# Attention with a computed position bias and two MLPs: scores in four PSUM banks, bias rows in runs of 512 columns

## The chip, the core and the metric

The kernel runs on one core of a Trainium2 chip. The metric is the device time of one execution in microseconds (us), from the first to the last instruction with the launch around it, as the median of several runs. The profile is one more execution of the same program, taken by the hardware profiler; its span is the time from its first to its last instruction.

The engines are TensorE (PE; its weight loads are listed apart as PEld), VectorE (DVE), ScalarE (ACT), GpSimd (POOL) and SyncE (SP), which issues the DMAs. Each engine works through its own queue in order.

## The reference

Attention over 2 batches, 8 heads, 576 positions and a head size of 64, with a bias that a small network makes of the distance of two positions; then two MLPs of 512 to 2048 to 512 over the 1152 tokens.

```python
scores = scale * np.matmul(q, k.transpose(0, 1, 3, 2))
x = (log1p(abs(pos[:, None] - pos[None, :])) / log1p(max(pos[:, None], 1)))[..., None]
bias = np.maximum(x @ w1 + b1, 0.0) @ w2            # hidden 32, one row per head
scores = scores + bias.transpose(2, 0, 1)[None]
attn = softmax(scores)                              # over the keys
x = (attn @ v), heads side by side: 1152 x 512
h = x @ w_in;  g = where(h > 0, h, exp(min(h, 0)) - 1);  x = g @ w_out      # first MLP
h = x @ w_in;  g = max(h, 0) + log1p(exp(-abs(h)));      x = g @ w_out      # second MLP
```

The MLP weights come as float64 and are turned into pairs of float32 parts on the chip. A product in full precision is made of three matmuls of split operands (high by high, high by low, low by high).

## The kernel before

**Attention.** The 576 query positions are worked in five blocks: first the last 64 positions of both batches together (block 0), then four blocks of 128 (blocks 1 to 4). A unit is one block, one batch and one pair of heads: 36 units, of which 4 belong to block 0. For a unit `scores` (L634) writes two 128x576 score tiles, `soft` (L667) adds the bias on DVE while it takes the maximum, `expo` does the exponential on ACT, `turn` transposes on PE, `e_hi` and `e_lo` split the result into two float16 parts, `av` multiplies by v, and the `fin_` steps normalise and split.

**Scores.** 576 columns of float32 are more than one PSUM bank (512 columns) holds. The tile `ps3` has three banks. The two heads of a unit use the upper and the lower 64 rows of the PE array side by side: head 0 writes 512 columns to bank 0, head 1 writes 512 to bank 2, and the 64 columns that are left of each go to the two ends of the middle bank (L658) in one full-height matmul of 128 columns, for which a zero-padded copy `kz` of the key tails is loaded (`load_tail`) and split (`z_hi`, `z_lo`). So a unit of blocks 1 to 4 is six matmuls of 64 rows by 512 columns in three pairs (L656) and three of 128 columns (L658). Block 0 has twice as many.

**Bias.** For eight groups s of 16 query rows in a block, four tiles `y` (L510 on POOL, L512 on DVE) hold the hidden layer, 576 columns each. `bias_mm` (L518) multiplies them by w2 in four column strips of the array, in two halves of 288 columns, into `pb`, two PSUM banks; `bias_ev` (L535) evicts 576 columns in one ACT instruction (L539) into one of two `sg` buffers; `bias_out` (L541) sends it by one DMA (L546) to the bias tile, which `soft` reads. Eight groups by four blocks make 32 of these; block 0 has four groups with a plainer form of `y` and matmul (L504, L506, L521).

**Weights.** While attention runs, DVE, ACT and POOL turn the first MLP's weights from float64 into two parts (L241 to L274), 32 half-tiles of 512 columns, and the MLP's matmuls (L1264, L1308) begin as soon as their first weights and rows are there.

**Order.** Every step is a task with an engine, a cost and dependences. A list `RANK` gives each task's priority; a planner (`Order.forward`) plays the engines through and writes the tasks out in the order that results, so each engine's queue, SP's too, is fixed when the program is built. The table `ON` says which engine does a task that two could do: `YP` the 144 `y` tiles, `WP` the first step of a weight half, `KHP`, `KG`, `QHP`, `QP` the splitting of k and q. `rotates("pb", 1)`, `rotates("sg", 2)` and `rotates("ps", 1)` say how many buffers there are of `pb`, `sg` and the score tile: a new group or unit may be written when the last reader of the buffer is done, which for the score tile are both `soft` steps of the unit before.

Of the kernel before, what the change touches and what calls it, by code (L numbers as in the profile page):

```python
# [157 lines left out]
]  # L158

HOLD = dict(A=0.10, V=0.11, G=18.49, T=0.00, D=19.64)  # L160

ON = dict(
    KHP="AVAVVVVAAA",
    KG="VVVVVVVVVV",
    QHP="VAAAAVVAVVAAVVVAAAAA",
    QP="VGVVGVVVVGGGVGGGGVGG",
    WP="GVVGGVGVVVGGGVVVVVGVVVVVGGGVVGVVGGVGVGGVGGVGVVVGVGGVGGVGVVGVGVGG",
# [1233 lines left out]
```

## Time and profile before

| | us |
|---|---|
| median of 3 runs | 591.74 (591.17 to 592.08) |
| the profiled execution | 593.84 |
| its span | 592.1 |
| PE busy in the span | 572.1 (97%) |
| DVE busy | 436.6 (74%) |
| ACT busy | 408.0 (69%) |
| POOL busy | 117.7 (20%) |

The shares of the whole span are averages over stages that differ: attention with the bias and the weights fills about the first 190 us, and from about 190 us on the MLP matmuls run. A stretch has to be looked at by itself, engine by engine. A PE that is listed as busy is not thereby at its peak, since pipelined matmuls overlap: what a matmul costs is the distance from its start to the next one's start.

### The profile page before, as it was taken

Reading aid. Unit: us, or ns where it says so; the run is one execution under the profiler, and the core shown is the slowest. Engines: PE = TensorE matmul, PEld = TensorE weight load, DVE = VectorE, ACT = ScalarE, POOL = GpSimd, SP = SyncE. Lnnn points to the kernel's source line nnn. Section 1 sums busy time; section 2 is a strip of 40 time slices with the busy share of each in tenths; the row PEclk is TensorE's granted clock in tenths of the full one; section 3 lists DMA queues with packets and bytes.
Section 4 is the critical chain, followed back from the end, with each engine's and each line's share of the span. In section 5 each row is a group of like instructions: output and inputs, shape, how many; then the busy total and the mean of one; then the engine's idle time right before and its main releaser. Section 6 shows DMA issues by size and latency. Waiting matters only on the chain.

```text
span 592.1 us, 12610 instructions
## 1 busy us (share of the span) xinstructions
PE 572.1 (97%) x5002; PEld 491.4 (83%) x5002; DVE 436.6 (74%) x872; ACT 408.0 (69%) x798; POOL 117.7 (20%) x159
## 2 busy tenths in 40 slices
PE   8489999999999999999999999999999999999997
PEld 5256777777878888888889999998888888899996
DVE  7799999899999999999974699999972222332222
ACT  7678798888997766767745777687865444565453
POOL 3047767648300010010200020211110000000000
PEclk9989999999999999999999999999999999999999
DMA  8842843315201444444450045434500000020001
GB/s 303 260 115 77 217 116 104 82 42 168 63 2 41 139 130 156 143 151 142 148 164 1 2 148 169 144 110 145 161 15 1 0 1 1 0 108 1 0 2 53
DMA packets 19355, 56.63 MB, mean 96 GB/s; under 512 B 2144, under 2 KB 2528, under 8 KB 19040
## 3 DMA queue, kind: packets, MB, share of 16 engines
q1 hardware_dynamic: 19296, 55.82, 30.9%
q8 instruction: 39, 0.64, 0.4%
q14 instruction: 20, 0.16, 0.1%
HBM read 41.66 MB, written 2.36 MB: 74 GB/s over the span
## 4 chain that ended last, share of the span: by engine, by line
PE 85%; DMA 5%; ACT 4%; DVE 4%; issue 1%; POOL 0%; SPq 0%; DVEq 0%; ACTq 0%; POOLq 0%
PE ph L1264 33%; PE ps L1308 33%; PE tp L702 5%; PE ps L656 4%; PE pa L727 4%; PE pb L527 3%; DMA vr<-in_vt_dram 2%; PE ps L658 2%; DMA bias<-sg 1%; DVE y L512 1%; DVE et L711 1%; DVE e L672 1%; ACT e L689 1%; ACT sg L539 1%; ACT et L706 1%
## 5 line engine op out<-in xcount | busy, mean ns | idle before, releaser
L1264 PE MATMUL ph<-xh,wh 128*128 128x512 f32 (+2 forms) x384 | 127.6, 332 | 0.5 <-DVE t L1280 0.4
L1264 PE MATMUL ph<-xl,wh 128*128 128x512 f32 (+2 forms) x384 | 127.2, 331 | 0.0
L1264 PE MATMUL ph<-xh,wl 128*128 128x512 f32 (+2 forms) x384 | 127.1, 331 | 0.0
L1308 PE MATMUL ps<-g,wh 128*128 128x256 f32 (+2 forms) x384 | 94.3, 332 | 0.5 <-DVE xl L1316 0.5
L1308 PE MATMUL ps<-wh,g 128*128 128x512 f32 x288 | 91.9, 385 | 0.0
L1282 DVE SCALAR_TENSOR_TENSOR t<-ph,t 128x512 f32<-128x512 f32 (+2 forms) x48 | 26.7, 557 | 88.0 <-ACT t L1276 87.9
L510 POOL TENSOR_SCALAR y<-tpk,nbp 128x576 f32<-128x576 f32 x88 | 73.4, 849 | 34.8 <-PE pb L527 28.7
L1264 PEld LDWEIGHTS ph<-xh,wh 128*128 128x128 f32 x384 | 72.1, 188 | 5.9 <-DVE t L1280 0.5
L1264 PEld LDWEIGHTS ph<-xl,wh 128*128 128x128 f32 x384 | 72.1, 188 | 5.0
L1264 PEld LDWEIGHTS ph<-xh,wl 128*128 128x128 f32 x384 | 72.1, 188 | 4.8
L249 POOL TENSOR_SCALAR w<-w 128x512 f32<-128x512 f32 x30 | 28.4, 946 | 227.1 <-ACT w L241 164.7
L1308 PEld LDWEIGHTS ps<-g,wh 128*128 128x128 f32 x384 | 66.6, 188 | 5.6 <-DVE xl L1316 0.7
L1289 DVE TENSOR_TENSOR g<-t,g 128x512 fp32r<-128x512 f32 (+2 forms) x96 | 57.1, 596 | 18.6 <-ACT g L1286 17.7
L1286 ACT CAST g<-t 128x512 fp32r<-128x512 f32 (+2 forms) x96 | 48.9, 510 | 27.9 <-DVE t L1282 15.7
L1308 PE MATMUL ps<-g,wl 128*128 128x512 f32 (+2 forms) x192 | 63.5, 331 | 0.0
L1308 PEld LDWEIGHTS ps<-wh,g 128*128 128x128 f32 x288 | 54.0, 187 | 10.3
L1274 ACT ACTIVATE t<-ph 128x512 f32<-128x512 f32 (+2 forms) x48 | 23.6, 492 | 56.2 <-PE ph L1264 56.1
L711 DVE SCALAR_TENSOR_TENSOR et<-tp,et 128x512 f16<-128x512 f32 x81 | 54.0, 682 | 3.9 <-ACT et L706 3.6
L689 ACT ACTIVATE e<-e,mx 128x576 f32<-128x576 f32 x72 | 55.5, 775 | 1.3 <-DVE mx L672 1.2
L1308 PE MATMUL ps<-wl,g 128*128 128x512 f32 x144 | 55.5, 385 | 0.0
L706 ACT ACTIVATE et<-tp 128x512 f16<-128x512 f32 x81 | 46.2, 595 | 12.2 <-PE tp L702 11.6
L702 PE MATMUL tp<-ident,e 128*128 128x128 f32 x324 | 46.6, 278 | 3.3 <-DVE et L711 1.6
(137 smaller groups left out, 1050.2 us busy)
## 6 DMA issues: line engine op xcount, KB each, us to landing
r<-in_wa_dram SPq DMA_DIRECT2D x32, 512.0 KB, 3.7
r<-in_wb_dram SPq DMA_DIRECT2D x32, 512.0 KB, 3.6
bias<-sg SPq DMA_DIRECT2D x32, 288.0 KB, 3.4
vr<-in_vt_dram SPq DMA_DIRECT2D x2, 1152.0 KB, 11.5
sp<-sg SPq DMA_DIRECT2D x8, 288.0 KB, 3.3
out_dram<-o SPq DMA_DIRECT2D x9, 256.0 KB, 2.0
kr<-in_kt_dram SPq DMA_DIRECT2D x4, 512.0 KB, 8.7
qr<-in_qt_dram SPq DMA_DIRECT2D x8, 256.0 KB, 5.4
```

The costliest lines, as they stand in the source:

```text
L249: eng.tensor_scalar(wf, wf, F64_HUGE, F64_TINY, op0=ALU.min, op1=ALU.max)
L510: eng.tensor_scalar(y, tpk[:, b0 : b0 + S], BIG, nbp[:, qd : qd + 1], op0=ALU.min, op1=ALU.max)
L656: nc.tensor.matmul(sc[:, 1024 * x : 1024 * x + 512], q[r], kp[n][r, bb, hp], start=i == 0, stop=i == last)
L689: nc.scalar.activation(e, e, AF.Exp, bias=mxs[u][:, x : x + 1], scale=-1.0, accum_out=sums[u - hp][:, h : h + 1])
L702: nc.tensor.transpose(tp[:, r], e[:, t * P : (t + 1) * P], ident)
L706: nc.scalar.activation(et[:, 0], tps[g, k].rearrange("p t i -> p (t i)"), AF.Copy, scale=2.0**14)
L711: nc.vector.scalar_tensor_tensor(et[:, 1], tp, 2.0**14, et[:, 0], op0=ALU.mult, op1=ALU.subtract)
L1264: nc.tensor.matmul(in_fours(ps), a[:, kk], in_fours(x[:, kk]), start=n == 0, stop=n == 3 * KT - 1)
L1282: nc.vector.scalar_tensor_tensor(t[0], ps, 0.0, t[0], op0=ALU.max, op1=ALU.add)
L1286: nc.scalar.copy(g[0], t[0])
L1289: nc.vector.tensor_sub(g[1], t[0], g[0])
L1308: self.nc.tensor.matmul(in_fours(self.acc(m, c, j)), a, in_fours(x), start=f == 0 and n == 0 and not two, stop=f == FT - 1 and n == 2 and ...
```

## The change

1. The score tile becomes two tiles `ps4` of two banks each. Each head's 576 columns are two halves of 288, one per bank. `kz`, `load_tail`, `z_hi` and `z_lo` go; `kp` holds all 576 columns of the keys, and each key load is 1152 columns wide instead of 1024. A unit of blocks 1 to 4 is now twelve matmuls of 64 rows by 288 columns, in six pairs.
2. `pb` shrinks from two banks to one; scores and `pb` together hold five banks as before. In blocks 1 to 4 the rows of the eight groups, 8x576 columns, are laid end to end and cut into nine runs of 512 (`PIECES`): runs 0 and 8 are one piece each, runs 1 to 7 two pieces (64+448, 128+384, 192+320, 256+256 and back). `y`, the matmuls, the eviction and the DMA are issued once per piece. Block 0 keeps its four groups, in halves of 288 columns with an eviction of each half.
3. The eviction may be on ACT or on DVE: a new table `EV` puts 30 of the 36 runs on ACT, 6 on DVE.
4. `RANK`, `HOLD` and `ON` are solved anew, with new costs. Of the `y` tiles of blocks 1 to 4, DVE has 41 of 144 (40 of 128 before) and POOL 103 (88). Of the first weight steps DVE has 26 of 64 (34), of the five-block q splits (`QHP`) ACT has 18 of 20 (12). `turn_round`, the planner's cost of a change between score, bias and other matmuls, now counts it for scores on leaving too.

Three places show how the instructions stand. SP's queue at the start, first before, then after (`kr` are key loads, `ktr` the key tails, `vr` the two loads of v, `sg` outs of block 0's bias rows):

```order
L342 DMA ktr_107<-in_kl_dram 128x512
L342 DMA ktr_109<-in_kl_dram 128x512
L354 DMA vr<-in_vt_dram 128x2304
L351 DMA sp_101<-in_tab_dram 128x512
L333 DMA kr_235<-in_kt_dram 128x1024
L333 DMA kr_237<-in_kt_dram 128x1024
L333 DMA kr_241<-in_kt_dram 128x1024
L546 DMA bias_200<-sg_0_243 16x8x576 x2
L354 DMA vr<-in_vt_dram 128x2304
L546 DMA bias_200<-sg_1_298 16x8x576 x2
```

```order
L358 DMA vr<-in_vt_dram 128x2304
L355 DMA sp_102<-in_tab_dram 128x512
L345 DMA kr_220<-in_kt_dram 128x1152
L345 DMA kr_230<-in_kt_dram 128x1152
L345 DMA kr_234<-in_kt_dram 128x1152
L358 DMA vr<-in_vt_dram 128x2304
L567 DMA bias_195<-sg_0_236 16x8x576 x2
L567 DMA bias_195<-sg_1_301 16x8x576 x2
```

The second load of v stood behind the first bias rows, which wait for an eviction; it now stands ahead of all of them, and the two tail loads are gone.

ACT in the middle of attention, before and after (`sg` the evictions, `et` the float16 parts, `e` the exponentials):

```order
L706 ACTIVATE et_2_2275<-tp_2_2197 128x512
L539 ACTIVATE sg_5_2281<-pb,bcst,inv 128x576
L706 ACTIVATE et_3_2300<-tp_3_2284 128x512
L764 CAST xh_72<-pr_2295 128x4x128
L689 ACTIVATE e_2290,sm_1958<-e_2290,mx_2289 128x576 x2
L539 ACTIVATE sg_6_2378<-pb,bcst,inv 128x576
```

```order
L557 ACTIVATE sg_5_1729<-pb,bcst,inv 128x320
L557 ACTIVATE sg_5_1729<-pb,bcst,inv 128x192
L693 ACTIVATE e_1672,sm_1607<-e_1672,mx_1671 128x576
L710 ACTIVATE et_7_1809<-tp_7_1777 128x512
L693 ACTIVATE e_1783,sm_1607<-e_1783,mx_1782 128x576
L557 ACTIVATE sg_6_1825<-pb,bcst,inv 128x384
L557 ACTIVATE sg_6_1825<-pb,bcst,inv 128x128
```

An eviction is two instructions now where it was one, three or four other instructions apart as before.

DVE just ahead of block 1's first `soft`, before and after (`y` the hidden layer's tiles, `et` the low float16 parts):

```order
L512 TENSOR_SCALAR y_990<-tpk,nbp 128x576
L711 SCALAR_TENSOR_TENSOR et_5_923<-tp_5_888,et_5_923 128x512
L583 TENSOR_TENSOR q_988<-qr_1_382,q_987 128x256
L555 CAST q_987<-qr_1_382 128x256
L711 SCALAR_TENSOR_TENSOR et_6_1011<-tp_6_997,et_6_1011 128x512
```

```order
L715 SCALAR_TENSOR_TENSOR et_4_942<-tp_4_903,et_4_942 128x512
L559 TENSOR_SCALAR sg_7_1003<-pb,inv,bcst 128x448
L559 TENSOR_SCALAR sg_7_1003<-pb,inv,bcst 128x64
L523 TENSOR_SCALAR y_8_3_1070<-tpk,nbp 128x512
L523 TENSOR_SCALAR y_0_0_1075<-tpk,nbp 128x512
```

DVE has an eviction of block 1 and the first `y` tiles of block 2 there, where it had two splits of q.

The core of the diff:

```diff
-HOLD = dict(A=0.10, V=0.11, G=18.49, T=0.00, D=19.64)
+HOLD = dict(A=0.25, V=0.08, G=15.09, T=0.00, D=26.34)
+    EV="AAAAAAAVAAAAVAAAAAAAAAAAAAVAAVAAVAAVA",
...
+PIECES = [
+    [(s, k0, k1, 576 * s + k0 - 512 * j)
+     for s in range(max(j - 1, 0), min(j + 1, 8))
+     for k0, k1 in ((max(512 * j - 576 * s, 0), min(512 * j + 512 - 576 * s, 576)),) if k0 < k1]
+    for j in range(9)
+]
...
-    for b in range(B):
-        load_tail(b)
...
+    def bias_y(eng, bi, j, c):
...
+        for s, k0, k1, o in PIECES[j]:
+            qd = (BLOCKS[bi] + 16 * s + 4 * c) // 4
+            yo, tk, nb = y[:, o : o + k1 - k0], tpk[:, 575 - 4 * qd + k0 : 575 - 4 * qd + k1], nbp[:, qd : qd + 1]
...
-    pb = psb.tile([P, 2, 512], F32, name="pb")[:, :, :SH]
+    pb = psb.tile([P, 512], F32, name="pb")
...
+        for _, k0, k1, o in PIECES[j]:
             for ps, (w, half) in enumerate(((w2h, 1), (w2h, 0), (w2l, 1))):
                 for c in range(4):
                     nc.tensor.matmul(
-                        pb[32 * c : 32 * c + 32, n],
+                        pb[32 * c : 32 * c + 32, o : o + k1 - k0],
                         w,
-                        ys[bi, s, c][:, n * SH : (n + 1) * SH, half],
+                        ys[bi, j, c][:, o : o + k1 - k0, half],
...
-        nc.scalar.activation(sgs[bi, s].rearrange("p (a j) -> p a j", a=2), pb, AF.Identity, bias=sh, scale=sc)
+            if eng is nc.scalar:
+                eng.activation(sg, p, AF.Identity, bias=bcst, scale=sc)
+            else:
+                eng.tensor_scalar(sg, p, sc, bcst, op0=ALU.mult, op1=ALU.add)
...
+        for s, k0, k1, o in PIECES[j]:
+            nc.sync.dma_start(bts[bi][s::8, :, k0:k1], sg[:, o : o + k1 - k0])
...
-    kp = [kq.tile([P, B, HP, 512], F32R, name=f"k{x}") for x in range(2)]
-    kz = [kq.tile([P, B, HP, P], F32R, name=f"kz{x}") for x in range(2)]
+    kp = [kq.tile([P, B, HP, S], F32R, name=f"k{x}") for x in range(2)]
...
-        for i, (q, n, bb) in enumerate(prods):
-            for x in range(2):
-                r = slice(64 * x, 64 * x + 64)
-                nc.tensor.matmul(sc[:, 1024 * x : 1024 * x + 512], q[r], kp[n][r, bb, hp], start=i == 0, stop=i == last)
-        for i, (q, n, bb) in enumerate(prods):
-            nc.tensor.matmul(
-                sc[:, 512:1024].rearrange("p (a j) -> p a j", a=8)[:, ::7],
...
+        for i, (q, k) in enumerate(prods):
+            for n in range(2):
+                for x in range(2):
+                    r = slice(64 * x, 64 * x + 64)
+                    nc.tensor.matmul(
+                        ps_of(x)[:, n], q[r], k[r, n * SH : (n + 1) * SH], start=i == 0, stop=i == len(prods) - 1
+                    )
...
-    t = 0.097 if last != kind and (last == "b" or kind in ("b", "s")) else 0.0
+    t = 0.097 if last != kind and (last in "bs" or kind in "bs") else 0.0
...
-        self.ps3 = pool.tile([P, 3, 512], F32, name="ps3")
+        self.ps4 = [pool.tile([P, 2, 512], F32, name=f"ps4{x}") for x in range(2)]
```

## Rows read from the trace of the kernel before

**Rows 1.** Busy time of the engines by stretch: from:to, length, then busy us.

```profile
0.00:20.00 20.00, 15.12 (x122) 10.03 (x122) 15.19 (x46) 16.41 (x26) 4.55 (x19) 1.00 0.90 307
20.00:40.00 20.00, 13.37 (x150) 8.69 (x154) 16.17 (x36) 11.84 (x18) 5.33 (x7) 0.83 0.62 170
60.00:180.00 120.00, 118.87 (x1987) 92.88 (x1987) 111.08 (x245) 104.98 (x222) 65.22 (x88) 1.00 0.35 96
180.00:220.00 40.00, 39.40 (x374) 33.62 (x371) 39.14 (x74) 29.37 (x57) 2.85 (x5) 1.00 0.34 106
220.00:300.00 80.00, 80.00 (x468) 71.14 (x468) 76.73 (x146) 54.26 (x102) 7.62 (x8) 1.00 0.47 148
```

**Rows 2.** The chain that ended last, around the start of the bias blocks: start, us, what.

```profile
11.29 14.45 DMA vr<-in_vt_dram
63.73 0.73 ACT sg L539
```

**Rows 3.** Timeline of PE over one score unit and one bias group: start, length, instructions.

```profile
144.47 0.97 PE L656 MATMUL ps<-k,q 64*128 64x512 f32 x6
145.38 0.55 PE L658 MATMUL ps<-kz,q 128*128 128x128 f32 x3
145.77 1.06 PE L702 MATMUL tp<-ident,e 128*128 128x128 f32 x8
146.75 0.44 PE L527 MATMUL pb<-y,w2h 128*32 128x288 f16 x8
147.64 0.51 PE L656 MATMUL ps<-k,q 64*128 64x512 f32 x2
```

**Rows 4.** Timeline of PE where full-height matmuls of 512 and 256 columns follow.

```profile
223.69 0.39 PE L1264 MATMUL ph<-xh,wh 128*128 128x512 f32 x1
...
226.37 0.27 PE L1264 MATMUL ph<-xh,wh 128*128 128x256 f32 x1
...
227.73 0.40 PE L1306 MATMUL ps<-xh,zero 128*128 128x512 f32 x1
```

**Rows 5.** Timeline of the weight loads over the unit of rows 3.

```profile
144.47 0.53 PEld L656 LDWEIGHTS ps<-k,q 64*128 64x128 f32 x6
145.38 0.41 PEld L658 LDWEIGHTS ps<-kz,q 128*128 128x128 f32 x3 [0.37 <-issue]
```

**Rows 6.** Groups of instructions by shape: count, then busy us, mean ns, idle before.

```profile
L539 ACT ACTIVATE sg<-pb,bcst,inv 128x576 f32<-128x576 f32 x32 | 26.6, 830 | 8.6 <-PE pb L527 4.3 <-issue 1.9 <-DMA bias<-sg 1.8
L1286 ACT CAST g<-t 128x512 fp32r<-128x512 f32 x32 | 19.8, 618 | 12.3 <-DVE t L1282 7.6 <-DVE t L1280 4.3
L1286 ACT CAST g<-t 128x256 fp32r<-128x256 f32 x32 | 12.9, 404 | 9.6 <-DVE t L1280 4.8 <-DVE t L1282 4.6
L711 DVE SCALAR_TENSOR_TENSOR et<-tp,et 128x512 f16<-128x512 f32 x81 | 54.0, 682 | 3.9 <-ACT et L706 3.6
L249 DVE TENSOR_SCALAR w<-w 128x512 f32<-128x512 f32 x34 | 14.7, 433 | 0.2 <-ACT w L241 0.2
```

**Rows 7.** Timelines of SP and DVE in the first 30 us: when issued, and what DVE waited for.

```profile
9.98 1.27 SPq L546 DMA_DIRECT2D bias<-sg  x2
11.29 0.59 SPq L354 DMA_DIRECT2D vr<-in_vt_dram  x1
...
28.20 0.16 DVE L599 TENSOR_TENSOR vm<-vm 128x2 f32<-128x2 f32 x1 [2.91 <-ACT vh L591]
```

**Rows 8.** Waits: who waited for whom, us in total, times, longest; the first from 0 to 300 us, the other 60 to 187.

```profile
PE pb L527 <- ACT sg L539: 3.5, 2, 3.3
...
DVE e L672 <- PE ps L658: 4.5, 14, 0.7
```

**Rows 9.** PE's first MLP matmul; DVE: the fifth weight tile's first half; its first matmul.

```profile
187.31 0.47 PE L1264 MATMUL ph<-xh,wh 128*128 128x512 f32 x1
...
211.92 0.68 DVE L274 TENSOR_TENSOR wl<-w,wh 128x512 fp32r<-128x512 f32 x1
...
214.16 0.47 PE L1264 MATMUL ph<-xh,wh 128*128 128x512 f32 x1
```

More of the change, by code (lines that the diff above doesn't have):

```diff
@@ L513, in bias_y @@
-        ys[bi, s, c] = y.bitcast(F16).rearrange("p (n two) -> p n two", two=2)
-    pb = psb.tile([P, 2, 512], F32, name="pb")[:, :, :SH]
-    def bias_mm(bi, s):
-        for n in range(2):
-            if bi == 0:
-                for c in range(4):
-                    nc.tensor.matmul(
-                        pb[32 * c : 32 * c + 32, n], w2f, ys[bi, s, c][:, n * SH : (n + 1) * SH], start=True, stop=True
-                    )
-                continue
+        k = qd - k0
+        if c < NACT:
+            eng.activation(y, lts[0][:, b0 : b0 + S], AF.Relu, bias=b1p[:, k : k + 1], scale=w1k)
+        else:
+            eng.tensor_scalar(y, lts[0][:, b0 : b0 + S], w1k, nb1p[:, k : k + 1], op0=ALU.mult, op1=ALU.max)
@@ new lines, in first_y @@
+        ys[bi, s, c] = y
+    def bias_y(eng, bi, j, c):
+        if bi == 0:
+            first_y(eng, bi, j, c)
+            return
+        y = erl.tile([P, S], F32, tag="y", name=f"y{bi}_{j}_{c}", bufs=NYB)
+        for s, k0, k1, o in PIECES[j]:
+            qd = (BLOCKS[bi] + 16 * s + 4 * c) // 4
+            yo, tk, nb = y[:, o : o + k1 - k0], tpk[:, 575 - 4 * qd + k0 : 575 - 4 * qd + k1], nbp[:, qd : qd + 1]
+            if eng is nc.gpsimd:
+                eng.tensor_scalar(yo, tk, BIG, nb, op0=ALU.min, op1=ALU.max)
+            else:
+                eng.tensor_scalar_max(yo, tk, nb)
+        ys[bi, j, c] = y.bitcast(F16).rearrange("p (n two) -> p n two", two=2)
@@ L525, in bias_mm @@
+    pb = psb.tile([P, 512], F32, name="pb")
+    def bias_mm(bi, j, n):
+        if bi == 0:
+            for c in range(4):
+                nc.tensor.matmul(
+                    pb[32 * c : 32 * c + 32, :SH], w2f, ys[bi, j, c][:, n * SH : (n + 1) * SH], start=True, stop=True
+                )
+            return
+        for _, k0, k1, o in PIECES[j]:
             for ps, (w, half) in enumerate(((w2h, 1), (w2h, 0), (w2l, 1))):
@@ L771, in attention @@
     bts[0] = bias_tile("bias0")
-    t_k, t_q, t_z = {}, {}, {}
-    for b in range(B):
-        dk = tq.done(9.5)
-        h = add(pick("KHP", 2 * HP + b, A=0.53, V=0.33), lambda e, b=b: z_hi(e, b), [dk])
-        lo = add(pick("KG", 2 * HP + b, G=1.22, V=0.6), lambda e, b=b: z_lo(e, b), [h])
-        t_z[b] = [h, lo]
-        r_et.append(([dk], [h, lo]))
+    t_k, t_q = {}, {}
     for hp in range(HP):
-        dk, rd = add(D_, 1.3, lambda e, hp=hp: load_k(hp), [], lat=1.7) if hp else tq.done(7.8), []
+        dk, rd = add(D_, 1.45, lambda e, hp=hp: load_k(hp), [], lat=1.7) if hp else tq.done(7.8), []
         for b in range(B):
-            h = add(pick("KHP", 2 * hp + b, A=0.53, V=0.33), lambda e, b=b, hp=hp: k_hi(e, b, hp), [dk])
-            lo = add(pick("KG", 2 * hp + b, G=1.22, V=0.6), lambda e, b=b, hp=hp: k_lo(e, b, hp), [h])
+            h = add(pick("KHP", 2 * hp + b, A=0.573, V=0.37), lambda e, b=b, hp=hp: k_hi(e, b, hp), [dk])
+            lo = add(pick("KG", 2 * hp + b, G=1.36, V=0.67), lambda e, b=b, hp=hp: k_lo(e, b, hp), [h])
             rd += [h, lo]
@@ L840, in attention @@
     late = [dq[1, b] for b in range(B)]
-    for bi, s in ((bi, s) for bi in range(len(BLOCKS)) for s in range(8 if bi else 4)):
+    for bi, s in ((bi, s) for bi in range(len(BLOCKS)) for s in range(9 if bi else 4)):
         yy = []
         for c in range(4):
-            eng = {A: 0.77} if bi == 0 and c < NACT else pick("YP", 4 * len(t_out) + c, V=0.43, G=0.72)
+            if bi == 0:
+                eng = {A: 0.77} if c < NACT else pick("YP", 4 * len(t_out) + c, V=0.45, G=0.75)
+            else:
+                n = len(PIECES[s])
+                eng = pick("YP", 4 * len(t_out) + c, V=0.33 + 0.06 * n, G=0.56 + 0.1 * n)
             yy.append(add(eng, lambda e, bi=bi, s=s, c=c: bias_y(e, bi, s, c), t_tab if bi else [tq.done(4.4)]))
@@ L847, in attention @@
                 t_y0.append(yy[-1])
-        mms = [add(T, 0.788 if bi else 1.1, lambda e, bi=bi, s=s: bias_mm(bi, s), yy + ([t_w2] if bi else []), kind="b")]
-        evs = [add(A, 0.73, lambda e, bi=bi, s=s: bias_ev(bi, s), mms)]
-        r_pb.append((mms, evs))
-        out = add(D_, 1.4 if bi else 1.9, lambda e, bi=bi, s=s: bias_out(bi, s), evs, lat=0.8 if bi else 1.58, free=not bi)
+        mms, evs = [], []
+        for n in range(1 if bi else 2):
+            mms.append(add(T, 0.72 if bi else 0.55, lambda e, bi=bi, s=s, n=n: bias_mm(bi, s, n), yy + ([t_w2] if bi else []), kind="b"))
+            m = len(PIECES[s])
+            eng = pick("EV", len(t_out) - 4, A=0.42 + 0.255 * m, V=0.55 + 0.07 * m) if bi else {A: 0.492}
+            evs.append(add(eng, lambda e, bi=bi, s=s, n=n: bias_ev(e, bi, s, n), mms[n:], free=True))
+            r_pb.append((mms[n:], evs[n:]))
+        out = add(D_, 0.3 + 0.5 * len(PIECES[s]) if bi else 2.9, lambda e, bi=bi, s=s: bias_out(bi, s), evs, lat=0.8, free=not bi or len(PIECES[s]) > 1)
         for y in yy:
@@ L865, in attention @@
         bs = (b,) if b is not None else range(B)
-        dep = [t for bb in bs for t in t_k[bb, hp] + t_z[bb] + t_q[bi, bb, hp]]
-        t_sc[u] = add(T, 1.9 if bi == 0 else 1.0, lambda e, u=u: scores(u), dep, kind="s")
+        dep = [t for bb in bs for t in t_k[bb, hp] + t_q[bi, bb, hp]]
+        t_sc[u] = add(T, 1.58 if bi == 0 else 0.79, lambda e, u=u: scores(u), dep, kind="s")
         for x in range(2):
-            dep = [t_sc[u]] + [t_out[bi, s] for s in range(8 if bi else 4)]
+            dep = [t_sc[u]] + [t_out[bi, s] for s in range(9 if bi else 4)]
             t_so[u, x] = add(V, 0.677, lambda e, u=u, x=x: soft(u, x), dep, free=True)
-            for s in range(8):
+            for s in range(9):
                 if (bi + 2, s) in t_out:
```

104 lines of the change are left out of this document (41 added, 63 removed), and 196 rows, old and new, of the table RANK.

## Prediction, made before the changed kernel was run

> **What bounds the kernel now.** I read the busy times by stretch first [rows 1]. From 60 to 180 us PE is busy 118.9 of 120 us, from 220 to 300 us all 80 of 80; from 0 to 40 us it is busy 28.5 of 40. So PE sets the pace from about 60 us on, and before that something else does. DVE runs close behind: 111.1 of 120, 39.1 of 40 between 180 and 220 us, 76.7 of 80. A stretch in which two engines are that full gives back only part of what one of them saves. ACT has 15 us free in the 120, POOL 55.
>
> The start hangs on the loads of v. SP issues the second one at 11.29 us, behind block 0's first bias rows [rows 7]; it lands 14.45 us later [rows 2], and DVE then stands 2.91 us for the work that ACT does on it [rows 7].
>
> Where attention ends, the MLP's matmuls are fed with little in hand: the fifth weight tile's first half is done at 211.92 + 0.68 = 212.6 us, and its first matmul starts at 214.16 [rows 9]. That is 1.6 us of room.
>
> **The score units.** A unit lasts from 144.47 to 145.77, 1.30 us [rows 3]: 0.91 for three steps of 512 columns and 0.39 for three of 128. In a stream of matmuls 512 columns cost (226.37 - 223.69)/12 = 0.223 us and 256 columns (227.73 - 226.37)/12 = 0.113 [rows 4], so a column is 0.43 ns and 288 columns 0.127. The three wide steps would be 0.67 in a stream; the other 0.24 is what entering and leaving the half-height form costs. Twelve matmuls in six pairs are then 6 x 0.127 + 0.24 = 1.00 us, 0.30 less. Thirty-two units: 9.6 us.
>
> Some of that comes back. The 128-column steps take 0.39, of which three loads at their spacing make 0.33 (three loads in 0.41, each about 0.19, so 0.11 apart [rows 5]); the other 0.06 is a first load that nothing hides. It falls on the next group now, in the 27 units that a full-height group follows: 1.6. Net 8.0 us.
>
> Block 0's four units have twice the products, so some 0.6 each, 2.4 together. They lie between 20 and 55 us, where PE has time to spare [rows 1]: 0 in the sum, 2.4 as the far end.
>
> **The bias groups.** One takes 147.64 - 146.75 = 0.89 us [rows 3]: six steps of 288 columns, 0.76, and 0.13 for the change of form. The columns of a block stay the same (9 x 512 = 8 x 576), and so does the number of steps, 48. A ninth group adds 0.13 per block, 0.5 in all. The short pieces are uncertain: two of 64 and two of 128 columns per block, three steps each. If they stream, nothing is added; if a step is never shorter than 0.11, the spacing of loads [rows 5], they cost 3 x (2 x 0.08 + 2 x 0.055) = 0.8 per block, 3.2 in all. So 0.5 to 3.7; I take 2.4, nearer the upper end, since four loads stand before each step. Both orders also count out how often PE goes from full height to scores or bias: 39 times before, 46 after. Seven times half of 0.24 is 0.8.
>
> PE's sum: 8.0 - 2.4 - 0.8 = 4.8 us less.
>
> **Evictions.** ACT's cost per column is (618 - 404)/256 = 0.84 ns [rows 6]. One eviction of 576 columns takes 0.73 in the chain [rows 2], so 0.25 is fixed, and two pieces of 512 together cost 0.43 + 0.50 = 0.93. Thirty runs on ACT (24 in two pieces, six in one at 0.68) are 26.4 us against 32 x 0.73 = 23.4, block 0's halves add about 1, six more q splits on ACT some 2: 6 us more, less 1.5 for key copies that go to DVE. ACT's 15 free us hide that. DVE's six evictions cost about 4 (0.6 to 0.7 each, like L711 with its PSUM source [rows 6]); eight first steps of the first MLP's weights that leave it give back 8 x 0.43 = 3.4 [rows 6], and the q and key splits come out a little lower. I take DVE as even. POOL gets 15 more `y` tiles and eight weight steps, about 20 us, which its 55 free us hide; what it costs if they don't is a late `y`, for which PE waits.
>
> With one bank a group may not start until the last one's eviction is through: 0.93 plus about 0.15 on each side, 1.2 us. In the order after, five of 35 gaps between bias groups hold less PE work than that, short by 2.5 us in all; two such gaps stood before, where PE waited 3.5 us [rows 8]. No change in the sum.
>
> **The start.** The second load of v no longer waits for an eviction, and ahead of it in the queue lie 0.51 MB of tails and 0.58 MB of bias rows less, 0.25 MB of wider keys more. At the 307 GB/s of the first 20 us [rows 1], 0.84 MB are 2.7 us. Against it block 0's evictions come in halves, each with its own way from PE to ACT and back: four more of some 0.3, and 0.25 more fixed time each, 2.2 us on ACT. DVE's stop of 2.91 us [rows 7] is the most that I would count: from 3 gained to 2 lost. I take 1 gained.
>
> **Sum.** 4.8 + 1.0 = 5.8 us. DVE keeps part: with 1.6 us in hand at the fifth weight tile [rows 9] and DVE's total unchanged, PE would arrive there 5 us early and find the weights missing. But DVE itself stood 4.5 us waiting for scores, 14 times [rows 8], and much of that goes with shorter units. I take 1.3 off: 4.5 us. From the profiled execution's 593.8 that is 589.3; it stands 2.1 above the median, so from the median, 591.7, I predict **587.2**.
>
> **Two rules beside this.** PE's six loads of a unit are through in 0.53 us [rows 5]; one after another at 0.11, each 0.19 long, they would take 0.74. So the two loads of a pair run at once. The Trainium skill (TensorE: Matmul & The Clock Gate, LDWEIGHTS) says that a load takes as long with few rows as with 128, so that cutting the height in half saves no load time. By that rule, if loads stood in one line, twelve loads of 107 ns, an estimate from that page, would be longer than the columns they hide behind, and the change would lose; the trace speaks for pairs.
>
> A group's eviction takes as long as the matmuls that fill the bank, 0.93 against 0.89. The Trainium skill (TensorEngine Tiling (Array Packing), PSUM Bottleneck) warns that tiling speeds up PE and not the emptying of PSUM, which may become the bottleneck, and advises using both engines for it. By that the third rival below would be the outcome; so far the trace shows two waits of that kind.
>
> **Rivals.** *More than I forecast.* Short pieces stream, block 0's shorter units count, v comes 3 us earlier: 8.0 - 0.5 - 0.8 + 1 + 3 = 10.7, say 9 to 10: 582. For it: PE idles 11.5 us in the first 40. Against: DVE's 97% from 180 on [rows 1].
>
> *DVE is the bound.* PE's saving becomes waiting for `soft` and weights, and only the start's 1 us is left, or nothing: 590.7, between 589.5 and 592.5. For it: the 1.6 us, DVE even. Against: DVE's waits for PE [rows 8].
>
> *The single bank holds PE up (slower).* Evictions are queued behind exponentials and copies on ACT. If they start on average 0.5 us later than I count, the gaps below 1.75 us fall short by 5.7 us; at 1 us, those below 2.25 by 12.9. From about 0.7 us on the gain is gone; at 1 us the time is about 595 to 598. For it: one bank, two instructions per eviction, ACT 87% busy. Against: 3.5 us of such waits so far [rows 8], most gaps at 1.8 to 3.7.
>
> *Loads don't hide behind 288 columns (slower).* Two loads of 0.11 in a row per pair make a step 0.22 and a unit 1.56, 0.26 more than now: 32 x 0.26 + 1.6 + 3.2 - 1 = 12 us, about 603. Against: a unit's six loads are through in 0.53 us [rows 5].
>
> The change does what it says on PE, but four banks don't let two units overlap: the next unit still waits for both `soft` steps.
>
> **Chances.** My forecast (584 to 589.5) 0.50, more 0.13, DVE 0.21, single bank 0.11, loads 0.05. About 0.2% (1.2 us) is what a measurement of this kernel can tell from no change. Faster: 0.50 + 0.13 + 0.09 of DVE's = 0.72. Same: 0.12 from DVE's. Slower: 0.16. The range leaves out the loads, half of the single bank and the far end of "more": 582 to 594.
>
> **What would show it.** A unit of twelve matmuls at 1.00 us from its start to the next group's (1.3 or more: loads); a bias group of two pieces at 0.8 to 1.0; PE's waits on `sg` at 3 to 5 us up to 300 us (10 or more: the single bank); `vr` landing by 23 us and DVE's stop ahead of `vm` below 1 us; the first MLP matmul at about 181 to 183 us instead of 187.3 [rows 9], with the fifth tile's weights still within 2 us of their use. I am wrong if PE's busy share from 60 to 180 us falls below 96% while the unit does shrink: then the time has gone to DVE or ACT.

## The result, and the profile after

The changed kernel takes 598.5 us (597.8 to 599.3) against 591.7, 1.0106 of before with an interval of 1.0076 to 1.0136: by that ratio 6.3 us slower (6.8 between the medians), where 4.5 us less was predicted. The profiled execution took 599.3 us, its span 597.5. All ratios here and below are of runs in the faster of the kernel's two states; one run, 597.0 us of the first kernel with whole groups, was in the slower one and is left out.

Busy time by stretch, as in [rows 1] (PE, PEld, DVE, ACT, POOL, then the granted clock):

```profile
20.00:40.00 20.00, 13.69 (x113) 6.92 (x113) 13.96 (x32) 13.49 (x23) 7.16 (x7) 0.81 0.46 124
40.00:60.00 20.00, 18.36 (x296) 14.04 (x295) 19.88 (x52) 14.71 (x33) 13.37 (x23) 0.85 0.36 104
60.00:180.00 120.00, 113.61 (x2107) 89.71 (x2107) 114.22 (x257) 103.77 (x230) 92.97 (x179) 1.00 0.40 107
220.00:300.00 80.00, 80.00 (x470) 71.08 (x467) 76.01 (x137) 54.78 (x101) 11.54 (x15) 1.00 0.45 145
```

The kernel before, from 40 to 60 us:

```profile
40.00:60.00 20.00, 17.66 (x336) 12.94 (x329) 18.73 (x37) 17.03 (x34) 15.32 (x17) 1.00 0.35 91
```

From 60 to 180 us PE is busy 113.6 us, 94.7%, where it was 118.9: below the 96% that I had named as the sign that time has gone elsewhere. DVE is full from 40 to 60 us (19.9 of 20, with 52 instructions where it had 37), and POOL is busy 93 us in the 120 where it was 65.

PE's timeline (start, length, instructions): block 1's second unit, one unit in the middle of attention with the transposes behind it, the first MLP matmul, and the fifth weight tile's first:

```profile
70.30 0.40 PE L666 MATMUL ps<-k,q 64*128 64x288 f32 x1 [0.28 <-DVE mx L676]
...
148.00 1.06 PE L666 MATMUL ps<-k,q 64*128 64x288 f32 x12
148.99 0.66 PE L706 MATMUL tp<-ident,e 128*128 128x128 f32 x4
...
193.50 0.47 PE L1268 MATMUL ph<-xh,wh 128*128 128x512 f32 x1
...
219.93 0.46 PE L1268 MATMUL ph<-xh,wh 128*128 128x512 f32 x1
```

A unit does take 0.99 us. But block 1's second unit starts at 70.30 us; before, it stood at 62.79:

```profile
62.79 0.97 PE L656 MATMUL ps<-k,q 64*128 64x512 f32 x6
```

The first MLP matmul starts at 193.50 against 187.31 [rows 9]. From there to the end of the span it is 404 us in either trace (597.5 - 193.5, 592.1 - 187.3). So 7.5 us are lost by 70 us, and the long stretch behind it gives back 1.3 (123.2 against 124.5), not 4.8. The loss has two places to look at: the start, and whatever takes the gain away.

The chain that ended last, of after, over the start (start, us, what):

```profile
6.82 2.53 POOL y L509
...
16.93 6.31 POOL y L509
...
64.73 4.59 DMA sp<-sg
```

The load of v, 14.45 us of [rows 2], is gone from the chain. In its place stand two `y` tiles of block 0, which POOL makes; the kernel before has both on DVE at about 0.6 us. The third row is the last write of block 1's bias rows. It lands at 69.3 us; before, it landed at 61.0:

```profile
57.36 3.67 DMA sp<-sg
```

Block 1's first `soft` on DVE needs these rows, and block 1's second unit waits for that `soft`: it runs at 69.48 us, before at 61.30. So what makes block 1's bias rows late makes the second unit late.

Groups of instructions, with the columns of [rows 6]: DVE's and POOL's `y` of blocks 1 to 4 over the whole trace, first before (one form each), then after with all forms of a line together and DVE's evictions, then the widest and the narrowest form of after on either engine:

```profile
L512 DVE TENSOR_SCALAR y<-tpk,nbp 128x576 f32<-128x576 f32 x40 | 24.0, 623 | 1.0 <-PE pb L527 0.8
L510 POOL TENSOR_SCALAR y<-tpk,nbp 128x576 f32<-128x576 f32 x88 | 73.4, 849 | 34.8 <-PE pb L527 28.7 <-DVE et L711 5.5
```

```profile
L523 DVE TENSOR_SCALAR y<-tpk,nbp 128x64 f32<-128x64 f32 (+7 forms) x73 | 28.9, 454 | 0.1
L521 POOL TENSOR_SCALAR y<-tpk,nbp 128x192 f32<-128x192 f32 (+7 forms) x183 | 96.8, 551 | 17.5 <-PE pb L538 13.2 <-issue 3.8
L559 DVE TENSOR_SCALAR sg<-pb,inv,bcst 128x448 f32<-128x448 f32 (+4 forms) x12 | 5.9, 531 | 0.0
```

```profile
L523 DVE TENSOR_SCALAR y<-tpk,nbp 128x512 f32<-128x512 f32 x9 | 4.9, 562 | 0.0
L523 DVE TENSOR_SCALAR y<-tpk,nbp 128x64 f32<-128x64 f32 x14 | 4.5, 325 | 0.0
L521 POOL TENSOR_SCALAR y<-tpk,nbp 128x512 f32<-128x512 f32 x23 | 17.3, 760 | 7.2 <-issue 3.8 <-PE pb L538 3.2
L521 POOL TENSOR_SCALAR y<-tpk,nbp 128x64 f32<-128x64 f32 x18 | 6.3, 348 | 0.7 <-PE pb L538 0.6
```

A piece of 64 columns takes DVE 0.325 us, one of 512 0.562: from these two widths 0.53 ns a column and 0.29 us fixed. On POOL 0.348 and 0.760 give 0.92 ns a column and 0.29 us fixed too. A tile in two pieces pays the fixed part twice. DVE has 4.9 us more of `y` (28.9 against 24.0, with 41 tiles for 40) and 5.9 of evictions. What PE waits for has changed with it. Waits from 60 to 180 us, before and then after (us in total, times, longest; PEld is the weight load that stands ahead of a matmul):

```profile
PEld ps L656 <- DVE mx L672: 2.8, 10, 0.5
PEld tp L702 <- DVE et L711: 1.1, 4, 0.3
```

```profile
PEld ps L666 <- DVE mx L676: 6.4, 8, 1.5
PEld tp L706 <- DVE et L715: 4.8, 14, 1.0
PE ps L666 <- DVE mx L676: 4.2, 7, 0.9
PE tp L706 <- DVE et L715: 1.6, 4, 0.7
```

Theory A: the two `y` of block 0 on POOL cost the start. Theory B: the second instruction of each tile in pieces fills DVE, or POOL, so that PE waits. Rivals: the single bank; the order of loads; block 0's evictions in halves.

### The profile page after: what moved, and what is told of

Read it like the earlier page. It is cut to its first block, busy times and chain, and to the rows that moved or that the text cites. A ratio compares the mean times of both kernels' runs of the same rounds, so it can differ in the third digit from the quotient of the medians.

```text
span 597.5 us, 13139 instructions
## 1 busy us (share of the span) xinstructions
PE 571.2 (96%) x5131; PEld 490.5 (82%) x5131; DVE 445.4 (75%) x898; ACT 412.4 (69%) x825; POOL 154.0 (26%) x266
## 4 chain that ended last, share of the span: by engine, by line
PE 80%; DVE 10%; DMA 3%; ACT 2%; POOL 2%; issue 2%; DVEq 0%; ACTq 0%
PE ph L1268 33%; PE ps L1312 33%; PE tp L706 4%; PE ps L666 4%; PE pa L731 3%; DVE e L676 3%; PE pb L538 2%; DVE et L715 2%; DVE y L523 2%; POOL y L509 1%; DMA bias<-sg 1%; DMA sp<-sg 1%; PE pb L531 1%; DVE vl L644 1%; ACT sg L557 1%
## 5 line engine op out<-in xcount | busy, mean ns | idle before, releaser
L521 POOL TENSOR_SCALAR y<-tpk,nbp 128x192 f32<-128x192 f32 (+7 forms) x183 | 96.8, 551 | 17.5 <-PE pb L538 13.2
L261 POOL TENSOR_SCALAR w<-w 128x512 f32<-128x512 f32 x38 | 31.4, 827 | 211.3 <-ACT w L253 187.1
L1293 DVE TENSOR_TENSOR g<-t,g 128x512 fp32r<-128x512 f32 (+2 forms) x96 | 55.5, 580 | 22.1 <-ACT g L1290 21.3
L715 DVE SCALAR_TENSOR_TENSOR et<-tp,et 128x512 f16<-128x512 f32 x81 | 52.8, 678 | 1.4 <-ACT et L710 1.1
L706 PE MATMUL tp<-ident,e 128*128 128x128 f32 x324 | 48.2, 284 | 2.8 <-DVE et L715 1.6
```

The source lines that it names most:

```text
L261: eng.tensor_scalar(wf, wf, F64_HUGE, F64_TINY, op0=ALU.min, op1=ALU.max)
L521: eng.tensor_scalar(yo, tk, BIG, nb, op0=ALU.min, op1=ALU.max)
L706: nc.tensor.transpose(tp[:, r], e[:, t * P : (t + 1) * P], ident)
L715: nc.vector.scalar_tensor_tensor(et[:, 1], tp, 2.0**14, et[:, 0], op0=ALU.mult, op1=ALU.subtract)
L1293: nc.vector.tensor_sub(g[1], t[0], g[0])
```

## Experiments: block 0's two `y`

Ratios are to the kernel before, timed alongside; 0.001 is 0.6 us.

**The operation by itself.** Behind the last output of the changed kernel, POOL ran both forms of `y`, with DVE at other work beside it.

```diff
+    two: nc.gpsimd.tensor_scalar(y, z, s1, s2, op0=ALU.mult, op1=ALU.max)
+    one: nc.gpsimd.tensor_scalar(y, z, BIG, s2, op0=ALU.min, op1=ALU.max)
```

> The changed kernel with a tail behind its last output: on an otherwise idle chip POOL runs the form of block 0's y (128x576, multiply by one column, maximum with another) twice alone, the form of blocks 1 to 4 (minimum with a constant, maximum with a column) twice alone, and then each of them twice beside a row of DVE casts and twice beside a row of DVE subtractions. The trace of the changed kernel shows 2.53 and 6.31 us for the first form on POOL, and 0.75 to 0.83 for the second. Theory A (the form itself is dear on POOL): 2.5 us or more alone, and about the same beside DVE. Theory B (it is DVE beside it that makes it long): 0.7 to 1.0 us alone, 2.5 to 6 beside DVE, and the second form grows as much.

Its groups by shape on POOL (first the form with two columns, then the one with a constant and a column):

```profile
L220 POOL TENSOR_SCALAR tail<-tail 128x576 f32<-128x576 f32 x6 | 15.3, 2552 | 2.5 <-DVE w L293 2.0
L223 POOL TENSOR_SCALAR tail<-tail 128x576 f32<-128x576 f32 x6 | 6.6, 1093 | 0.4
```

The form itself is dear: 2.55 us on average, 2.5 beside casts and 2.85 beside subtractions, against 1.09. The two "alone" came while the MLP still ran, so an idle DVE was not had. The 6.31 us of the second tile in the changed kernel is not reached here and stays unexplained. It isn't fixed either: this kernel's own start is that of the changed one, and there the second tile takes 3.54 us:

```profile
17.00 3.54 POOL L535 TENSOR_SCALAR y<-sp,xs_first 128x576 f32<-128x576 f32 x1 [7.59 <-PE pb L557]
```

Its first MLP matmul comes at 188.89 us in place of 193.50. That is one execution of each, so starts that differ by a few us between two traces are to be read with care. The Trainium skill (GPSIMD Engine Reference, When to use GPSIMD) calls operations with one tensor as input roughly line-rate on this engine. By that the two forms, which read and write the same columns, would take about as long; measured, one takes 2.3 times the other.

**The planner as an obstacle.** The first try at moving these tiles changed the letters of the planner's table `ON`, in the kernel after and, the other way, in the one before.

```diff
-    YP="GVVGVVVVVVGV...
+    YP="GVVVVVVVVVVV...
```

> The changed kernel with the two y of block 0 that it gives to POOL (third of the first group, fourth in the trace's 6.8 to 9.3 and 16.9 to 23.2 us) on DVE, where the kernel before has them; nothing else differs. Theory A (these two hold up the bias rows of block 0 and with them all that follows until 70 us): 4 to 6 us less than the changed kernel, 592.5 to 594.5, no PE wait on POOL's y before 30 us, first soft of block 0 at 34 to 36 us in place of 39.9. Rival (the start is late for another reason, block 0's evictions in halves or the single bank, and the wait falls to the next): within 1.5 us of 598.5.

> The kernel before with the same two y of block 0 moved from DVE to POOL; nothing else differs. Theory A: 3 to 6 us slower than before, 595 to 598, with POOL at 2.5 to 6.3 us for each. Rival (the kernel before takes it in its slack ahead of the last load of v, 25.7 us): 591 to 593.

1.0056 (1.0032 to 1.0080) for the first, 1.093 for the second: 55 us slower. Neither is a clean step. The planner gives each task its time by the engine it stands on, and two other letters made it set the whole program in another order (ACT's instructions stand in another order within the first 60 us); with a `RANK` solved for other choices that order came out far worse in the second. From here on the planner sees the old letters, and the engine is changed where the instruction is issued.

**Order kept.**

```diff
-            first_y(eng, bi, j, c)
+            first_y(nc.vector if eng is nc.gpsimd else eng, bi, j, c)
```

> The changed kernel with its order of instructions kept on every engine, and only the two y of block 0 that POOL makes (6.8 to 9.3 and 16.9 to 23.2 us) handed to DVE at the place in DVE's order where they were planned. Theory A (these two cost the start): the bias rows of block 0 done some 4 us earlier, the first soft at 36 us or before in place of 39.9, and 3 to 6 us off the end: 592.5 to 595.5. Rival (late for another reason): within 1.5 us of 598.5.

> The kernel before with its order kept on every engine, and the same two y of block 0 (fourth of the first group, third of the third) handed from DVE to POOL, where they are the only work at that time. Theory A: slower than before by 1 to 5 us, since each takes 2.3 to 2.8 us on POOL in place of 0.5 to 0.6 on DVE and the group's matmuls wait. Rival (hidden behind the last load of v, which lands at 25.7 us): within 1 us of before.

The first: 1.0053 (1.0026 to 1.0080), 3.1 us back; block 0's first `soft` comes at 37.4 us in place of 39.9, not at 36 as expected. The second: 1.0011 (0.9984 to 1.0037), nothing, although POOL took 2.53 and 3.08 us there. So theory A holds for half of the loss. I read the pair as a trade: in the kernel before the late load of v hid such a delay; the changed order removed that wait, and its gain went to the next in line. No run has the one without the other.

## Experiments: the pieces

**Whole groups.** Each tile `y` and each eviction of blocks 1 to 4 becomes one instruction of 512 columns; the matmuls and the writes stay as they are. Such a kernel leaves out the second piece's own shift and scale, so its bias rows are not the reference's; it serves for the time alone, as do all kernels of this section with something whole.

```diff
-        for s, k0, k1, o in PIECES[j]:
+        for s, k0, k1, o in PIECES[j][:1]:
...
-            yo, tk, nb = y[:, o : o + k1 - k0], ...
+            yo, tk, nb = y[:, :512], ...
```

> As the one with block 0's two y on DVE, and in blocks 1 to 4 each group's y and its eviction are one instruction of 512 columns with the first piece's columns, in place of one for each piece (144 y in place of 256, 36 evictions in place of 64; the matmuls and the writes of the rows stay); rows of a second piece are therefore not those of the reference. Theory A (the pieces cost nothing, being hidden): the same as the one it is made from, within 1 us. Rival (the small pieces load DVE and POOL, and PE waits for them): 2 to 4 us less than that one, PE's busy share of 60 to 180 us back above 96%.

> The changed kernel, order kept, with each group's y and eviction in blocks 1 to 4 as one instruction of 512 columns with the first piece's columns (144 y in place of 256, 36 evictions in place of 64), so that rows of a second piece are not the reference's. The same edit took 4.4 us from the kernel with the start planned anew (594.9 to 590.5). Theory A (the pieces cost DVE and POOL time for which PE waits): 3 to 5 us less than the changed kernel, 593.5 to 595.5. Rival (what was lost in the start hides it): under 1.5 us.

> Both edits on the changed kernel, order kept: block 0's two y on DVE, and whole groups in blocks 1 to 4 (rows of a second piece are not the reference's). If the two losses are separate and together all that kept the gain from showing: 587 to 591, that is 2 to 5 us under the kernel before, which leaves the smaller score units their 8 us less the ninth groups' 2 to 4. If something else holds the stretch from 60 to 190 us: 591 to 595.

0.9968 (0.9943 to 0.9994) for the first, 0.0088 under the kernel with the same newly planned order, with PE busy 115.08 us from 60 to 180, 95.9% and not above 96; 1.0046 (1.0025 to 1.0068) for the second, 3.6 us under the changed kernel; 0.9976 (0.9957 to 0.9994) with both, 7.7 us under it. The two losses, 3.1 and 3.6 us alone, are separate and add up within the intervals. The last two kernels differ in block 0's two `y` only and repeat their price: 4.1 us (1.0046 to 0.9976).

**The order of loads.** The first load of MLP weights is tied to the eighth write of block 1's rows; there are nine now, and SP issues 512 KB ahead of the last. That could be why the last write is late. The chain of after shows it 4.59 us long, 5.95 in the kernel with block 0's `y` on DVE.

Here `W.dma` keeps its loads until the end of `bias_out(1, 8)`:

```diff
+        if (bi, j) == (1, 8):
+            late, W.late = W.late, None
+            for a in late:
+                W.dma(*a)
```

> The changed kernel with block 0's two y on DVE (595.3 in its run, 1.0053 of before), and one more step: SP issues the first load of MLP weights (512 KB) behind the ninth write of block 1's bias rows, not ahead of it; nothing else differs. In the traces that write lands 4.6 and 6.0 us after it begins, against 3.7 before, and block 1's first soft waits for it. Theory C (the eighth write is still taken for the last one, and the load ahead of the ninth delays it): the write lands in 2.5 to 4 us, PE's stop at 61 to 66 us shrinks by 1 to 3 us, and 1 to 3 us come off: 592.5 to 594.5. Rival (the two loads right behind it share the queues all the same, or PE's next wait takes over): within 0.8 us of that kernel.

1.0059 (1.0023 to 1.0095), against 1.0053: nothing in the time. In the two traces block 1's second unit comes at 66.87 us in place of 68.47, so a gain of up to 1.5 us is not excluded by intervals this wide. DVE was busy 20.00 of the 20 us from 40 to 60 in both.

**Which part of the pieces.** On top of that kernel (block 0's `y` on DVE and the load behind, 1.0059): all six evictions that DVE makes on ACT; `y` whole but evictions in pieces; both whole; and `y` whole on one engine alone (the line with `whole` is POOL's; DVE's has `is not`).

```diff
-            if eng is nc.scalar:
-                eng.activation(sg, p, AF.Identity, bias=bcst, scale=sc)
+            if True:
+                nc.scalar.activation(sg, p, AF.Identity, bias=bcst, scale=sc)
...
+        whole = eng is nc.gpsimd
+        for s, k0, k1, o in PIECES[j][: 1 if whole else 2]:
```

> As the one with the load behind, and all evictions of blocks 1 to 4 on ACT: the six groups that DVE evicts are handed to ACT at their place in the order. Theory D (DVE is what PE waits for between 70 and 180 us): 1 to 2 us less than that kernel. Rival (ACT's pieces, 0.40 to 0.78 us each, then hold the single bank longer): 0 to 2 us more.

> As the one with the load behind, with each group's y alone in one instruction (evictions in pieces as in the changed kernel; rows of a second piece are not the reference's). If the 112 more y on POOL and DVE are what the pieces cost: 2.5 to 4.5 us less than with the load behind alone. If it is the 28 more evictions, which hold the single bank: under 1.5 us less.

> As the one with the load behind, with each group's y and eviction in blocks 1 to 4 in one instruction (rows of a second piece are not the reference's): 588 to 590, that is 3.5 to 4.5 us under the same without, as the pair of the fixed order gave (595.3 and 590.8). If less than 2: the pieces only cost where the late write had left PE waiting.

> The kernel with block 0's two y on DVE and the first weight load behind the ninth write (1.0059 of before), with the y that POOL makes in one instruction of 512 columns for each group, those of DVE in pieces as in the changed kernel (rows of a second piece are not the reference's). If POOL's y are what PE waits for: 1.000 or below, 3 to 5 us less. If DVE's are: 1.004 to 1.006.

> The same with DVE's y in one instruction for each group, and POOL's in pieces (rows of a second piece are not the reference's). If DVE's are the cost: 1.000 or below, with DVE under 19 us of the 20 from 40 to 60 us. If POOL's are: 1.004 to 1.006.

| against 1.0059 | ratio | interval |
|---|---|---|
| DVE's evictions on ACT | 1.0072 | 1.0042 to 1.0102 |
| POOL's `y` whole | 1.0041 | 1.0021 to 1.0062 |
| DVE's `y` whole | 1.0002 | 0.9983 to 1.0021 |
| all `y` whole | 0.9972 | 0.9943 to 1.0002 |
| `y` and evictions whole | 0.9945 | 0.9916 to 0.9975 |

Busy time by stretch with DVE's `y` whole, with everything whole, then with everything in pieces (1.0059), and with DVE's evictions on ACT:

```profile
40.00:60.00 20.00, 18.80 (x382) 13.61 (x380) 17.93 (x36) 14.35 (x31) 14.92 (x27) 0.99 0.39 107
```

```profile
60.00:180.00 120.00, 115.14 (x2092) 93.48 (x2088) 113.95 (x249) 106.94 (x232) 71.53 (x104) 1.00 0.34 97
```

```profile
60.00:180.00 120.00, 114.50 (x2070) 90.15 (x2066) 114.19 (x258) 105.95 (x236) 92.48 (x177) 1.00 0.38 106
```

```profile
60.00:180.00 120.00, 113.57 (x2060) 89.59 (x2053) 106.85 (x242) 107.44 (x242) 92.25 (x177) 0.99 0.38 105
```

The pieces' `y` cost 5.2 us (1.0059 to 0.9972), about two thirds of it DVE's; by the middle values POOL's give 1 us and the evictions 1.6, with intervals that overlap. DVE's load from 40 to 60 us falls from 20.00 to 17.93 with its own `y` whole. Handing DVE's evictions to ACT brings nothing, though DVE's busy time from 60 to 180 us falls from 114.19 to 106.85. So a lighter DVE in that long stretch is not enough; whether ACT's pieces took back a gain is not shown. With everything whole the first MLP matmul starts at 181.5 us, where I had expected it (181 to 183), and the kernel stands at 0.9945, 3.3 us under the one before.

The traces say where the time goes, one execution each (us):

| | block 1's second unit | first MLP matmul | between |
|---|---|---|---|
| before | 62.79 | 187.31 | 124.5 |
| changed | 70.30 | 193.50 | 123.2 |
| in pieces, 1.0059 | 66.87 | 190.10 | 123.2 |
| POOL's `y` whole | 63.93 | 188.01 | 124.1 |
| DVE's `y` whole | 63.36 | 187.48 | 124.1 |
| all `y` whole | 62.20 | 183.98 | 121.8 |
| `y` and evictions whole | 61.18 | 181.54 | 120.4 |

Most of what whole pieces bring, 5.7 of 8.6 us here, lies ahead of block 1's second unit, where DVE is full and block 1's bias rows are late. With one engine's `y` whole all of it lies there.

## Experiments: a version that computes everything

If a second instruction per tile is what costs, the columns can be cut so that there is none. Eight groups of a block hold the first 512 columns of one row each, and the first group holds the last 64 columns of all eight rows. Its `y` is one maximum of eight shifted windows of the table with eight columns repeated. Each group's matmuls are then 12 of 512 columns. These kernels, too, have block 0's `y` on DVE and the load behind.

```diff
+    def by_row(a, step, n):
+        return bass.AP(tensor=a.tensor, offset=a.offset, ap=[a.ap[0], [step, 8], [n, 64]])
...
+        if j == 0:
+            nc.vector.tensor_max(tails(y[:, :512]), by_row(tpk[:, b0 + 512 : b0 + 576], -16, 1), by_row(nbp[:, qd : qd + 1], 4, 0))
...
+            nc.vector.tensor_mul(tails(sg), tails(pb), by_row(sc, 1, 0))
+            nc.scalar.activation(sg, sg, AF.Identity, bias=bcst)
```

The first has this alone. The second has, on top, every other `y` of two groups of block 1 on POOL; the third, in place of that, all `y` of blocks 2 to 4 outside the tails on POOL and the tails' writes spread out, from a buffer of their own; the fourth, on top of the third, no eviction but the tails' on DVE.

> The same kernel with the 576 columns of a row cut the other way: eight groups of a block hold the first 512 columns of one row each, and the first group of the block holds the last 64 columns of all eight rows. Each y is then one instruction (that of the tails a maximum of eight shifted windows of the table with eight columns repeated, on DVE), each group 12 matmuls of 512 columns, and each eviction one instruction, but for the tails a DVE product with the eight scales and an ACT addition; eight writes of 64 columns for the tails. The whole output is computed. If the pieces' y and evictions are the cost: 588 to 591, 0.993 to 0.998 of before. If the tails' group (four y of 0.6 to 0.9 us on DVE at the block's start, eight writes of 0.5 us on SP) takes their place: above 1.000.

> As the one with the tails in one group, and in block 1's first two whole groups every second y on POOL in place of DVE. If DVE is full from 40 to 60 us and POOL has 6 to 8 us free there: 0.5 to 2 us less than that kernel. If POOL's longer 0.8 us holds the groups' matmuls: 0 to 1 us more.

> As the one with the tails in one group (1.0037 of before), with all whole y of blocks 2 to 4 on POOL (16 more, some 9 us less on DVE), and the eight writes of a block's tails issued one by one ahead of the other groups' writes, from a buffer of their own; the whole output is computed. If DVE's load is what is left: DVE 105 to 108 of the 120 us from 60 to 180 us, and 0.996 to 1.001. If the tails themselves are (four maxima and a product on DVE at a block's start, an addition on ACT): 1.002 to 1.004.

> As the last one (0.9979 of before), with the six evictions of blocks 1 to 4 that DVE makes (0.80 us each) on ACT (0.78 us each); the whole output is computed. If DVE's load is still what costs: 1 to 2 us less, 0.994 to 0.997 of before. If DVE is no longer what PE waits for: 0.997 to 0.999, the same within the measurement. In the kernel with y in pieces the same step gave nothing (1.0059 to 1.0072).

1.0037 (1.0016 to 1.0058), 1.0035 (1.0013 to 1.0058), 0.9979 (0.9955 to 1.0002), 0.9984 (0.9960 to 1.0008). Busy time from 60 to 180 us of the first and the third:

```profile
60.00:180.00 120.00, 112.64 (x1802) 84.37 (x1795) 115.55 (x247) 101.53 (x220) 68.17 (x99) 1.00 0.37 103
```

```profile
60.00:180.00 120.00, 114.08 (x1834) 86.51 (x1828) 111.97 (x239) 105.22 (x227) 76.65 (x113) 1.00 0.36 98
```

The first fell on the side against the idea: four maxima at 0.71 us and a product at 0.68 per block kept DVE as full as the pieces had, while POOL stood idle for 52 us. The second, where 0.5 to 2 us less was expected, brings nothing. Taking the plain tiles of blocks 2 to 4 to POOL brings 3.4 us, less than the 9 us of work that was moved would suggest, and DVE comes to 111.97 us, not to the 105 to 108 expected; the spread writes and their buffer were changed in the same run, and their share was not measured apart. In the fourth DVE comes down to 109.56 us in that stretch and the time stays. The last two stand 7.2 to 7.5 us under the changed kernel, and about 1 us under the one before, which their intervals do not tell from no change.

## Why the prediction was wrong

**The score units were right.** The unit of twelve is 0.99 us in the middle (1.00 predicted, 1.287 before), block 0's of 24 1.80 against 2.41 (0.6 less predicted). Thirty-two times 0.296 are 9.5 us. The rival on loads is out.

**The bias groups were priced too high.** A group takes 0.80 us in the middle, in pieces or whole, against 0.885: 36 x 0.80 = 28.8 us against 32 x 0.885 = 28.3, 0.5 more in place of 2.4. The short pieces stream, the lower end of my range. The 1.6 and 0.8 for loads and changes of form were not measured apart. So PE's own work fell by about 9 us without these two and by 6.6 with them as I put them, more than the 4.8 of my sum.

**The step that failed is the eviction paragraph.** "POOL gets 15 more `y` tiles" and "I take DVE as even" counted tiles. 144 tiles are 256 instructions, and each carries some 0.29 us besides its columns. On DVE 73 instructions stand for 41 tiles, 4.9 us more of `y` by the groups above, which the line never had; its evictions are 5.9 us, not about 4. I had worked the pieces out on PE and on ACT, and not on the two engines that make `y`. On ACT, too, they were cheap in the sum: 22 runs of two pieces and eight whole ones take 30.4 us, not 26.4, and two pieces of 64 and 448 columns 0.397 + 0.713 = 1.11, not 0.93. I had built on the 0.73 of one eviction in the chain, where the 32 of [rows 6] take 0.83 on average. What the runs show in its place: the pieces' `y` cost 5.2 us of time, in the traces most of it ahead of 67 us, where DVE is full, and their evictions 1.6 by the middle values. A price was to be had from the rows: DVE's L711 and L249 of [rows 6] have one width each, but ACT's two widths there leave a fixed 0.19 us. The Trainium skill (VectorE: DVE Perf Modes, The TRN2 errata) says that instructions reading SBUF pay a fixed extra time each, and advises tiles of 512 elements or more; the trace agrees, with 0.325 us for 64 columns against 0.562 for 512. It would have been the reason to count instructions.

**POOL's cover was real and DVE's was not.** POOL's `y` grew by 23.4 us (73.4 to 96.8), close to my 20 by luck, since I put the pieces at nothing and took more weight steps. Its pieces cost about 1 us of time by the middle values, which the intervals do not tell from nothing. For DVE I took 1.3 us off, and the measured price was 3.4 for its `y` alone.

**The single bank was right.** The groups of blocks 1 to 4 wait 2.6 us for an eviction up to 300 us, in two waits (3.5 in two, [rows 8]). With block 0's groups it is 6.8 us against 8.7 before, less with one bank than with two; I had named 10 as the sign against me. Waits of PE from 0 to 300 us, first of block 0's groups, then of the others; the last fence has block 0's before:

```profile
PE pb L531 <- ACT sg L551: 4.2, 5, 1.7
...
PE pb L538 <- ACT sg L557: 1.5, 1, 1.5
...
PE pb L538 <- ACT sg L551: 1.1, 1, 1.1
```

```profile
PE pb L521 <- ACT sg L539: 5.2, 3, 2.4
```

**The start was wrong too.** The second load of v is issued at 7.89 us and lands 12.1 later, at 20 us in place of 25.7, more than the 2.7 us earlier that I had counted by bytes, and DVE's stop ahead of `vm` is gone as predicted. But I took 1 us gained, at most 2 lost, and 3.1 were lost to two `y` that POOL makes. The order of POOL's queue and the table `YP` show them; I had read the table for blocks 1 to 4 alone, and no row of the trace before has that form on POOL. Block 0's evictions in halves were not tried apart; PE waits for them 4.2 us in all, where it waited 5.2 for whole ones, so the traces show no loss by them.

**What DVE keeps in the MLP.** The fifth tile's first matmul comes 26.4 us after the first (26.9 before, [rows 9]): nothing there waited longer. The stretch behind the first MLP matmul is 404 to 405 us before and after, so the 1.3 us that I took off there were not lost there.

**The rivals.** "DVE is the bound" named the mechanism, at 0.21, and its price was too small: I let it eat the gain and no more. The change also costs, because it puts work on DVE. Altogether, from 1.0106: 0.0053 for block 0's `y`, 0.0087 for the pieces' `y`, 0.0027 for their evictions, nothing for the load (1.0059 behind 1.0053), and 0.9945 is left, a gain of 3.3 us. That is still a third of PE's 9: with everything whole PE is busy 115.1 us from 60 to 180 (118.9 before), so part of its saving is waiting there. DVE is busy 113.95 (111.1 before), and the prediction's first paragraph would make it the reason; that is not shown, and the kernel with 106.85 us of DVE speaks against DVE's load alone. What holds PE there stays open.

## What to carry to other kernels

When a tile is cut into pieces, count the instructions on every engine that touches it, not only on the one that the change is for, and price each by its fixed part, stretch by stretch: an engine that is even over the whole may be full for the 20 us that matter. An engine chosen by a planner's table is to be priced by the form of the operation, since two forms on one engine can differ by a factor of two and more. When a wait is removed, ask what else may have been hiding behind it.

## What the hardware showed that was not expected

Beside POOL's two forms (2.55 against 1.09 us), PE's clock took a part in the start. The first score unit of block 0 behind 38 us runs at a granted clock of 0.50, the 1.2 GHz level, in the changed kernel; from 34 to 41 us PE was busy 4.92 of 7 us. The two stretches, then nearly all of the same unit with block 0's `y` on DVE, and with the load behind and everything whole:

```profile
34.00:41.00 7.00, 4.92 (x53) 3.42 (x51) 6.93 (x12) 5.58 (x12) 2.11 (x3) 0.87 0.47 126
40.69:44.55 3.86, 3.79 (x25) 3.19 (x25) 3.86 (x13) 2.53 (x6) 2.96 (x4) 0.50 0.39 107
```

```profile
38.89:42.06 3.17, 3.17 (x23) 2.90 (x23) 3.17 (x11) 1.45 (x4) 1.31 (x2) 0.50 0.68 187
```

```profile
35.76:37.59 1.83, 1.83 (x24) 1.66 (x24) 1.83 (x6) 1.83 (x5) 1.83 (x1) 1.00 0.10 22
```

In the changed kernel it takes 3.86 us; the next of the same form, at 47.05, takes 1.80. In the kernel before PE was busy 9.43 of 11 us from 34 to 45 at the full clock. Those 2 us lie ahead of the 70 us by which 7.5 are lost. Taking block 0's `y` off POOL does not bring the clock back in its trace; the kernel with everything whole has it. With both edits but the load not behind, the unit is again at 0.52, so no single cause of these 2 us is shown.
